# A batch of two for the first layer norm, with TensorE transposes and a newly searched order, in a two-layer linear-attention and GLU kernel

## The chip, the cores and the metric

The kernel runs on one core of one Trainium2 chip. The metric is device time in microseconds (us). A profile gives the *span* of one execution, about 2 us less than its time. Engines: PE is TensorE (PEld its weight loads), DVE is VectorE, ACT is ScalarE, POOL is GpSimd, SP issues transfers.

## The reference, cut to what matters

Four blocks in turn on a 2048 x 512 input: linear attention (A), a gated GLU (B), A, B, each behind a layer norm and with a residual. Only the first layer norm and the k-stage of the first A concern us.

```python
x = A_x                                          # [1, 2048, 512], bf16
x = x + _A_ref(_layernorm(x), A_wqkv, A_w_phi, A_wo)
x = x + _B_ref(_layernorm(x), B_W_gate, B_W_up, B_W_down)
...                                              # the same A and B once more
# in _A_ref, with 32 heads of 16:
pk = einsum("bhsd,hdf->bhsf", k, w_phi)
phi_k = concatenate([softmax(pk), softmax(-pk)])
kv = einsum("bhsf,bhsd->bhfd", phi_k, v)         # a sum over the whole sequence
```

The sum over the sequence is the point: until phi_k of all 2048 rows (16 tiles of 128) is there, no output of the attention can be made. The masked copy of kv, called *the KV matrix* below, ends the k-stage.

## The kernel before: the parts that matter

Every operation is recorded with what it reads and writes; a static order per engine (`ORDER`, found by an offline search) says which stands where, and `CHOICE` which engine takes an operation that could run on two. An engine works through its list in order, waiting on semaphores, so an operation that waits holds all behind it.

```python
for t in range(4):
    ldx(t, t + 1)                    # tiles 0 to 3, one load each
...
first = [r("x", 3)]                  # later loads wait until tile 3 has landed
ldx(4, 8, first)
ldx(8, 12, first)
...

def ln_stats(self, ts, tag):         # statistics of the tiles ts
    for t in ts:
        op("dve", ... e.bn_stats(k.stats6[:, t, :], k.x_sb[:, t, :]) ...)
        op("dve", ... e.bn_aggr(k.mv[:, t, :], k.stats6[:, t, :]) ...)
    # one "rv" and one reciprocal root for all of ts, on POOL
    op("pool", ... rv1[:, t0:t1] = var + eps ...)
    op("pool", ... rstd[:, t0:t1] = rv1 ** -0.5 ...)

def ln(self, t, tag, on_act=False, pe_bank=None, stats=True, copy_act=False):
    ...                              # ytile = x * rstd + nmr, on DVE or ACT
    if pe_bank is None:              # transpose by DMA
        self.dma_tr(... e.dma_start_transpose(k.yT[:, :, t*128:(t+1)*128], k.ytile[:, yb, :]) ...)
        return
    for c in range(NC):              # or four TensorE transposes into PSUM
        op("pe", ... e.transpose(pv[:, c*128:(c+1)*128], k.ytile[:, yb, c*128:(c+1)*128], k.ident[:]) ...)
    self.op2("act" if copy_act else "dve", ... copy of pv to yT ...)

def L(st):                           # a slab of four tiles
    self.ln_stats(tiles(st), "L0")
    for t in tiles(st):
        self.ln(t, "L0", on_act=t % 2, stats=False)
```

Tiles 0 to 3 are transposed on TensorE (`pe_bank` given), tiles 4 to 15 by DMA. After its tile is projected, k goes through two exponentials on ACT, a sum and a reciprocal on DVE (`Zk`, `rZk`), a product on POOL (`phik`), and is accumulated on TensorE (`kvacc`). TensorE fills waiting time with 70 dummy matmuls.

The softmax here doesn't subtract the row's maximum and nothing guards it: scores larger than these inputs give would overflow.

Of the kernel before, what the change touches and what calls it, by code (L numbers as in the profile page):

```python
# [14 lines left out]
        "29 26 6 25 27 28 2a 2b 4t 2c 39 49 3u 4y 4e 44 5i 5n 58 5s 4j 6j 6k 67 73 72 8l 6d 84 6a 4o 83 8k 91 9x 9y 7r 96 9z c4 c5 9b c6 9g d9 da db b4 f9 f8 "  # L15
        "fm fl ay ee ef b2 eg gz gy fz h0 hx hw fy ij g5 g4 ik gb ga gg gh ii hv mk mj n4 n3 mu mt lm lq lt ne nd nn no nt r8 o5 o4 rf of op oq jv kn p0 pa pb "
        "vg pl pw pv vk q6 qg qh qr s1 ko sd sc sn xw xt sx sy t8 lg tt tj ti zn u4 ue u3 zu up uo uz wd wo wp x9 wz xa m8 ru ym yn xk z7 11o z8 yx 10k 11s zi "
        "10l 11v 10v 142 w2 12t yb 149 146 134 13p 135 13f 109 159 14z 13q 15a 15u 12a 15v 15k 14o 16x 178 177 17i 1b7 16m 18l 1aw 1c9 1db 1ad 1by 1d0 1e6 1dv "
        "1ea 1f0 1fg 1ew 1em 1gj 1fw 1gk 1fc 1gi 1jm 1hk 1hl 1hj 1kb 1fs 1ib 1ic 1kr 1l7 1g8 1ia 1j2 1j3 1gx 1ll 1lk 1j1 1m9 1ma 1nv 1k6 1ob 1mz 1my 1lj 1or "
        "1l3 1kn 1p7 1nn 1m8 1mn 1no 1mx 1pl 1pk 1ly 1q9 1nm 1o7 1nc 1qa 1pj 1qz 1qy 1on 1rq 1rp 1q8 1s4 1p3 1qx 1s3 1py 1ro 1t5 1t6 1s5 1s6 1t8 1qn 1t7 1u7 "  # L20
        "1ua 1u8 1xr 1uw 1uv 1u9 1xx 1y3 1uy 1ym 1yn 1ux 1z1 1z2 1y9 1yl 1zh 1zg 1z0 1zv 1zw 1zf 24t 1zu 24u 255 24v 24w 256 258 230 257 25u 25t 25h 25i 25k "
        "25w 25v 25j 26q 271 27d 272 22j 27n 27c 27z 27o 27y 289 28a 28l 28k 28v 28w 297 29h 296 29i 29t 29s 2be 23c 23x 2bp 2bq 24i 2cc 2cb 2c1 26f 2c0 2dj "
        "2cn 2cm 2di 2dt 2b3 2e5 2du 2e4 2ef 2eg 2er 2eq 2ft 2fu 2hu 2i5 2i6 2ih 2ig 2j2 2ir 2j3 2a7 2is 2d7 2kg 2k6 2kh 2k5 2l2 2l3 2ks 2kr 2mh 2le 2mg 2ld "
        "2fi 2hb 2ju 2m5 2qa 2pz 2qb 2n8 2ql 2qw 2qx 2qm 2sa 2r7 2sl 2sb 2r8 2ny 2sw 2sx 2t7 2sm 2pg 2t8 2um 2tj 2ti 2ul 2g8 2rz 2mv 2ua 2vw 2x5 2ak 2v0 2xg "
        "2xr 2xh 2od 2y3 2xs 2y2 2vd 2yd 2yp 2ye 2yo 2z0 2zb 2yz 2zm 2za 2zl 2gl 2wo 2zw 2zx 308 2wb 307 30z 2oq 31c 30m 322 "),
    "dve": (
        "2z 30 33 3a 3b 3e 3l 3m 3v 3k 3w 3p 2m 53 3z 5d 5x 5z 5t 5v 5u 60 5y 5w 7i 7g 7f 7h 6l 64 6m ao 74 ap 75 an am 85 7t 86 8m a0 7x 8n 7v a3 a1 a4 c7 ca "
        "c8 cb dc df b0 fa dg fn dd fo fb eh ek el ei em h1 h2 fq h4 hy hz h5 i1 il im i0 in io j2 j1 j3 j4 ix jd iz je iy j0 k6 jj k7 ku ky l1 l2 jo l3 l4 jp "
        "l6 l7 lv lw ju kc ly lz nu kh rc rg ki rh og ld ri o6 le or p1 rk pc pm rl vn vo q7 m5 px vq qi m6 xp qs kp s2 vs so se r4 sz xy xz t9 rr tk tu y1 u5 "
        "uf uq zr 13s we lh v0 zw zx zy zz rs vc 13t vz x0 wq w0 y8 y9 xb yo xl 13v 106 107 17w yy 15x zj 15y m9 z9 17x 15z 10m 17y 1b9 1ba 19o 10w 12u 11y 181 "  # L30
        "19p 14c 120 121 136 118 14d 13g 16c 14e 16d 150 19r 1cb 127 11k 13r 15b w3 128 1cc 18b 18c 15w 15l 1cd 14l 14m 16y 16j 16k 17j 179 17v 18i 18j 1a3 1a4 "
        "1bo 1bp 19b 1cq 1cr 18z 1aa 1ab 1b8 1dl 1ax 1dm 19n 1bv 1cx 1bw 1cy 1ca 1e8 1ds 1dt 1e7 1eb 1dc 1ey 1fe 1f3 1fh 1d1 1en 1ex 1jk 1kp 1fu 1fx 1gl 1fj "
        "1ft 12b 1k9 1fd 1l8 1ks 1gy 1dw 1hm 1g9 1hn 1j4 1j5 1gm 1id 1ha 1go 1nt 1l5 1nw 1mb 1ie 1i1 1hp 1mc 1la 1o9 1is 1k7 1jj 1p5 1oc 1gn 1os 1op 1ko 1p8 "
        "1lm 1ln 1n0 1ig 1n1 1n2 1l4 1lo 1pm 1lz 1lp 1nd 1np 1mo 1j7 1nq 1pn 1po 1r0 1pp 1r1 1o8 1r3 1qb 1qc 1s7 1s8 1oo 1p4 1rr 1rs 1se 1sf 1pz 1qo 1t9 1tg "
        "1rf 1xp 1ta 1th 1qe 201 1xs 1sw 1xv 202 203 20f 1xu 1ty 1tl 204 20g 1y1 208 209 1yo 1um 1y7 1y6 1yp 1z3 1ya 1yq 1z4 1yc 1zi 1zj 1zl 1zx 1zy 200 1zz "
        "20a 21r 21q 21s 21p 20d 221 222 227 22u 22v 22c 23n 23o 22d 20m 22i 248 249 235 236 265 23b 20n 2et 26r 266 2gm 2eu 24f 23u 23v 273 2ev 27e 2gn 280 "
        "28b 27p 2at 24g 2au 28m 2go 2lg 298 2cx 29j 28x 29u 2cy 2j5 26c 2j6 26d 2n9 2na 2f8 2f9 2bf 23d 2a6 2lh 2br 2aj 2li 2ll 2b0 2h1 2cd 2c2 2h2 2d4 2ff "
        "2co 23y 2b1 2or 2os 2dk 2nc 2d5 2fg 2e6 2eh 2dv 2es 2tl 2fv 2jk 2jl 2g7 2ra 2ou 2b4 2hv 2rb 2i7 2ow 2lv 2tm 2lw 2gk 2it 2h8 2h9 2ii 2j4 2no 2m2 2k7 "
        "2np 2rf 2m3 2jr 2js 2l4 2ki 2kt 2p6 2p7 2lf 2mi 2mu 2rp 2nv 2nw 2rq 2n7 2m6 2u0 2u1 2qc 2q0 2hc 2jv 2op 2oc 2vm 2pd 2qn 2qy 2pe 2r9 2sc 2rw 2rx 2vn "
        "2t9 2sn 2sy 2tk 2un 2uz 2u7 2u8 2vt 2vu 2vc 2x6 2xt 2ub 2xi 2wa 2yf 2wn 2y4 2yq 2s0 2zn 2z1 2zy 2zc 309 30l 30y 31b 31o 320 "),  # L40
    "pool": (
        "2p 0 1 4 2t 5 2w 2x 31 2 2u 2n 2o 32 3c 34 3d 3n 3o 2y 3x 3y 3f 2s 2r 2q 2v 61 62 66 63 69 6c 3 7j 7l 7k 7m 7n 7o 6n 7p 7q 76 ar aq as au at 87 av aw "
        "ax 8o a2 a5 c9 cc dh fp fc de fd ff ej h3 fs en h6 l5 lu lx rj jw vp jx vr vt xx kq y0 zv y2 100 13u 13x 17z li 11w rv 160 11x 14a 14b ma 162 19q 1bb "
        "1be 11z 10a yc 19t 14f 1bc yd 1cg rw w4 1ce 10b 18m 14p 1ec 16n 1ed 1f1 1f2 1fi 1fy 1fz 1jn 1kc 1kd 1bz 18n 16o 1ke 14q 1jo 1kt 1jp 1c0 1ku 1l9 1ae "
        "1ho 12c 1nx 1p9 1dx 1pa 1if 1od 1md 1ny 1oe 1ot 1j6 1d2 1ou 1me 1n3 1af 1r2 1nr 1ns 1sg 1sj 1s9 1sc 1rt 1qd 1sa 1tb 1te 1tc 1xt 206 1sh 1ti 1tj 20h "
        "1y4 1y5 20k 1xy 1xz 1y0 1ru 1yr 1yb 1z6 1z5 1zk 20i 20b 20o 20r 20p 2ew 2gr 2gp 22k 22l 2ey 2j7 2j8 23e 26g 2ja 24j 2nb 24k 23z 2lj 2ot 2b5 2tn 2to "
        "2tq 2d8 26h 2ne 2rc 2rd 2d9 2hd 2fj 2fk 2nz 2o0 2jw 2vx 2ph 2m7 2s1 2pi 2uc 2vy "),
    "pe": (
        "7 8 9 a b c d e f g h i j k 4p 4q 4r 4s l m n o p q r s t u v w x y z 35 36 37 38 10 11 12 13 14 15 16 17 3g 3h 3i 3j 18 45 46 47 48 3q 3r 3s 3t 4z 50 "
        "51 52 59 5a 5b 5c 4u 4v 4w 4x 4a 4b 4c 4d 40 41 42 43 5e 5f 5g 5h 4f 4g 4h 4i 5j 5k 5l 5m 19 1a 1b 54 55 56 57 1c 1d 1e 5o 5p 5q 5r 1f 1g 6f 6g 6h 6i "  # L50
        "1h 6y 6z 70 71 1i 1j 1k 1l 1m 1n 1o 8g 8h 8i 8j 1p 1q 1r 1s 6p 1t 1u 7z 80 81 82 1v 1w 6o 1x 1y 1z 20 21 22 23 24 4k 4l 4m 4n 9l 9m 9n 9o 8x 8y 8z 90 "
        "9h 9i 9j 9k 9p 9q 9r 9s 9t 9u 9v 9w 6q 6r 6s 6t 77 78 79 7a 92 93 94 95 bo bp bq br bs bt bu bv 6u 6v 6w 6x 97 98 99 9a 88 89 8a 8b bw bx by bz c0 c1 "
        "c2 c3 ct cu cv cw 9c 9d 9e 9f cx cy cz d0 d1 d2 d3 d4 d5 d6 d7 d8 f4 f5 f6 f7 fh fi fj fk 7b 7c 7d 7e 8c 8d 8e 8f 8p 8q 8r 8s dy dz e0 e1 a6 a7 a8 a9 "
        "e6 e7 e8 e9 e2 e3 e4 e5 ea eb ec ed fu fv fw fx ae af ag ah cd ce cf cg cl cm cn co 8t 8u 8v 8w aa ab ac ad gm gn go gp gi gj gk gl ai aj ak al ch ci "
        "cj ck gq gr gs gt gu gv gw gx di dj dk dl g0 g1 g2 g3 hn ho hp hq dq dr ds dt ia ib ic id cp cq cr cs dm dn do dp hr hs ht hu g6 g7 g8 g9 du dv dw dx "
        "es et eu ev eo ep eq er gc gd ge gf ie if ig ih mb mc md me mf mg mh mi f0 f1 f2 f3 ew ex ey ez h7 h8 h9 ha hf hg hh hi i2 i3 i4 i5 ip iq ir is hb hc "
        "hd he hj hk hl hm i6 i7 i8 i9 it iu iv iw j5 j6 j7 j8 j9 ja jb jc mz n0 n1 n2 mv mw mx my k2 k3 k4 k5 jf jg jh ji jy jz k0 k1 ml mm mn mo mp mq mr ms "
        "kr ks kt kv kw kx kz l0 jk jl jm jn lj lk ll ln n5 n6 n7 n8 lo lp lr ls n9 na nb nc nf ng nh ni nj nk nl nm jq jr js jt k8 k9 ka kb r5 r6 r7 r9 np nq "
        "nr ns kd ke kf kg ob oc od oe o0 o1 o2 o3 nw nx ny nz ra rb rd re o7 o8 o9 oa ol om on oo oh oi oj ok l9 la lb lc os ot ou ov kj kk kl km p6 p7 p8 p9 "
        "p2 p3 p4 p5 vd ve vf vh ow ox oy oz m1 m2 m3 m4 pr ps pt pu pd pe pf pg pn po pp pq ph pi pj pk vi vj vl vm py pz q0 q1 q8 q9 qa qb q2 q3 q4 q5 qc qd "  # L60
        "qe qf qj qk ql qm xm xn xo xq rx ry rz s0 qn qo qp qq qt qu qv qw qx qy qz r0 r1 r2 r3 s8 s9 sa sb s4 s5 s6 s7 sf sg sh si xr xs xu xv sj sk sl sm sp "
# [295 lines left out]
ACT = mybir.ActivationFunctionType  # L357
# [19 lines left out]
CHOICE = {}  # L377
# [38 lines left out]
class Kernel:  # L416
# [96 lines left out]
    def setup(self):  # L513
        op, dma, r = self.op, self.dma, self.r
        k = self
# [698 lines left out]
```

## Time and profile before

| | |
|---|---|
| time, 3 executions | 379.43 us median (379.27 to 379.86) |
| span of the profiled one | 377.4 us |
| TensorE busy | 367.7 us, 97% of the span |
| statistic of tile 2 starts (DVE) | 6.94 us |
| first statistic of the second slab starts (DVE) | 10.99 us |
| KV matrix starts (DVE) | 53.07 us |

The prediction shows the busy tenths, the stretches and the waits. A line of a timeline gives start, duration, line, operation, output and input, count.

```profile
10.99 2.46 DVE L623 BATCH_NORM_STATS2 stats<-x_sb 128x6 f32<-128x512 bf16 x4
...
53.07 0.98 DVE L797 TENSOR_TENSOR kvbd<-ps,mask 128x136 bf16<-128x136 f32 x4
```

I call the first S and the second K. Between them VectorE has almost no wait; from K to the end of the span are 377.4 - 53.07 = 324.3 us.

### The profile page before, as it was taken

The numbers are of one execution on the slowest core, as the hardware profiler recorded it, in microseconds if no ns is written. First come the engines' busy times: TensorE is split into PE (matmuls) and PEld (weight loads), VectorE is DVE, ScalarE is ACT, GpSimd is POOL, SyncE is SP. The second block draws the span as 40 slices with busy tenths as digits, with TensorE's granted clock in tenths as the row PEclk, the third lists the DMA queues.
The fourth block names the chain that finished last, engine by engine and source line by source line (L and its number), as shares of the span: only waits on it lengthen the run. The fifth ranks groups of instructions, "written<-read, shape, count | busy, mean of one in ns | idle before, by whom it ended". The sixth has DMA issues, their size and how long they took to land.

```text
span 377.4 us, 6882 instructions
## 1 busy us (share of the span) xinstructions
PE 367.7 (97%) x2519; PEld 203.9 (54%) x2565; DVE 276.2 (73%) x607; ACT 227.0 (60%) x463; POOL 130.8 (35%) x234
## 2 busy tenths in 40 slices
PE   6999999999999999999999999999999999999997
PEld 5654555877744454454444446577664454445443
DVE  5999998989968676459799999898984654342323
ACT  3999878765744127874677568584635451653450
POOL 6799941133344001350463577023221201000020
PEclk9999999999999999999999999999999999999999
DMA  7632794313326444310300045335543442142012
GB/s 233 173 76 52 187 240 149 77 33 56 78 43 94 97 64 84 70 30 14 70 2 1 2 81 95 79 63 95 83 83 75 81 86 56 28 71 70 30 42 70
DMA packets 87856, 29.33 MB, mean 78 GB/s; under 512 B 79792, under 2 KB 86800, under 8 KB 87824
## 3 DMA queue, kind: packets, MB, share of 16 engines
q1 hardware_dynamic: 84368, 25.86, 33.7%
q10 hardware_dynamic: 3456, 3.05, 2.5%
q8 instruction: 20, 0.33, 0.4%
q14 instruction: 12, 0.10, 0.1%
HBM read 7.91 MB, written 2.10 MB: 27 GB/s over the span
## 4 chain that ended last, share of the span: by engine, by line
PE 85%; POOL 7%; DVE 3%; issue 2%; ACT 1%; DMA 1%; POOLq 0%; DVEq 0%
PE ps L962 37%; PE ps L1011 20%; PE ps L725 7%; PE ps L942 7%; POOL expk L750 5%; PE ps L822 5%; PE ps L988 3%; PE ps L921 2%; PE ps L787 1%; PE ps L886 1%; DMA hT<-in_A_wqkv_dram 1%; DVE Zk L744 1%; POOL rstd L648 1%; PE ps L868 1%; PE ps L539 0%
## 5 line engine op out<-in xcount | busy, mean ns | idle before, releaser
L962 PE MATMUL ps<-yT,Wgu 128*128 128x512 bf16 (+2 forms) x870 | 150.8, 320 | 0.6
L962 PEld LDWEIGHTS ps<-yT,Wgu 128*128 128x128 bf16 x880 | 78.5, 98 | 58.8 <-ACT expk L970 1.0
L964 ACT ACTIVATE gate_sb<-ps 128x512 bf16<-128x512 f32 (+2 forms) x110 | 50.7, 480 | 55.1 <-PE ps L962 41.8
L1011 PE MATMUL ps<-Wd,hT 128*128 128x512 bf16 (+4 forms) x354 | 79.3, 373 | 0.5
L1011 PEld LDWEIGHTS ps<-Wd,hT 128*128 128x128 bf16 (+1 forms) x363 | 34.6, 98 | 39.5 <-DVE hT L972 0.7
L972 DVE TENSOR_TENSOR hT<-gate_sb,expk 128x512 bf16<-128x512 bf16 (+2 forms) x70 | 23.9, 361 | 30.4 <-ACT expk L970 21.4
L970 ACT ACTIVATE expk<-ps 128x512 bf16<-128x512 f32 (+2 forms) x70 | 32.0, 475 | 22.2 <-PE ps L962 19.5
L710 ACT ACTIVATE sq<-x_sb,nmr 128x512 bf16<-128x512 bf16 x48 | 34.6, 721 | 10.3 <-DVE x_sb L687 6.6
L744 DVE TENSOR_REDUCE Zk<-expk 128x64 f32<-128x1024 bf16 x32 | 38.1, 1203 | 1.0 <-ACT expk L737 0.7
L714 POOL TENSOR_TENSOR rstd<-rv,mone 128x1 f32<-128x1 f32 x32 | 18.6, 589 | 50.2 <-DVE rv L712 50.0
L1013 DVE SCALAR_TENSOR_TENSOR x_sb<-ps,rstd,x_sb 128x512 bf16<-128x512 f32 (+2 forms) x33 | 23.9, 728 | 16.1 <-PE ps L1011 13.5
L942 PE MATMUL ps<-wo_p,oT 128*128 128x512 bf16 x118 | 30.8, 379 | 0.6 <-DVE oT L413 0.3
L975 DVE TENSOR_TENSOR hT<-gate_sb,ps 128x512 bf16<-128x512 bf16 (+2 forms) x40 | 21.7, 544 | 12.6 <-ACT gate_sb L964 6.4
L855 POOL TENSOR_TENSOR expq<-expq,rho 128x256 bf16<-128x256 bf16 x36 | 22.2, 624 | 24.4 <-DVE rho L852 23.7
L847 DVE TENSOR_REDUCE Zq<-expq 128x64 f32<-128x1024 bf16 x24 | 28.8, 1204 | 0.8 <-POOL rho L852 0.5
L687 DVE SCALAR_TENSOR_TENSOR x_sb<-ps,x_sb 128x512 bf16<-128x512 f32 x32 | 21.9, 687 | 8.6 <-PE ps L942 7.8
L750 POOL TENSOR_TENSOR expk<-expk,rZk 128x1024 bf16<-128x1024 bf16 x13 | 25.9, 2005 | 0.6 <-DVE rZk L746 0.6
L755 POOL TENSOR_TENSOR expk<-expk,rZk 128x512 bf16<-128x512 bf16 x17 | 19.1, 1134 | 11.8 <-DVE rZk L746 11.5
L822 PE MATMUL ps<-Wqp,yT 128*128 128x512 bf16 x91 | 22.8, 379 | 0.3
L725 PE MATMUL ps<-Wkp,yT 128*128 128x512 bf16 x84 | 22.0, 379 | 0.2
L725 PE MATMUL ps<-wv_p,yT 128*128 128x512 bf16 x85 | 21.9, 379 | 0.2
L712 POOL TENSOR_SCALAR rv<-rv 128x1 f32<-128x1 f32 x22 | 4.3, 203 | 45.3 <-ACT sq L710 45.3
(126 smaller groups left out, 514.1 us busy)
## 6 DMA issues: line engine op xcount, KB each, us to landing
out_dram<-x_sb ACTq DMA_DIRECT2D x15, 128.0 KB, 1.7
x_sb<-in_A_x_dram SPq DMA_DIRECT2D x3, 512.0 KB, 5.0
Wgu<-in_B_W_up_dram SPq DMA_DIRECT2D x4, 344.0 KB, 5.5
Wgu<-in_B_W_gate_dram SPq DMA_DIRECT2D x4, 344.0 KB, 4.3
Wd<-in_B_W_down_dram SPq DMA_DIRECT2D x5, 256.0 KB, 3.3
yT<-ytile SPq DMA_TRANSPOSE x56, 2.5
qT<-expq SPq DMA_TRANSPOSE x40, 2.5
x_sb<-in_A_x_dram SPq DMA_DIRECT2D x4, 128.0 KB, 3.6
```

What stands on the lines that cost most here:

```text
L710: op("act", lambda e: e.activation(k.sq[:], k.x_sb[:, t, :], ACT.Square, scale=-float(D), bias=k.nmr[:, t, :], accum_out=k.rv1[:, t, :]), ...
L725: op("pe", (lambda ic, bank, W: lambda e: e.matmul(k.pb[bank][:], k.yT[:, ic, t * 128:(t + 1) * 128], W[:, ic, :], start=(ic == 0), stop=( ...
L744: op("dve", lambda e: e.tensor_reduce(k.Zk[:, zb, :], k.expk[:, t, :, :, :].rearrange("p g s (h f) -> p (g s h) f", f=16), AX.X, ALU.add), ...
L750: op("pool", lambda e: e.tensor_tensor(kv, kv, k.rZk[:, rb, :].unsqueeze(2).to_broadcast([P, 64, 16]), ALU.mult), [r("expk", t, 0), r("exp ...
L822: op("pe", (lambda ic, bank, tt: lambda e: e.matmul(k.pb[bank][:], k.yT[:, ic, tt * 128:(tt + 1) * 128], k.Wqp[:, ic, :], start=(ic == 0), ...
L847: op("dve", lambda e: e.tensor_reduce(k.Zq[:, b, :], k.expq[:, t, :, :, :].rearrange("p g s (h f) -> p (g s h) f", f=16), AX.X, ALU.add), ...
L942: op("pe", (lambda c, bank: lambda e: e.matmul(k.pb[bank][:], k.oT[:, ob, c, :], k.wo_p[:, c, :], start=(c == 0), stop=(c == NC - 1)))(c, ...
L962: op("pe", (lambda bank, W, ic, fc, Mf: lambda e: e.matmul(k.pb[bank][0:Mf, 0:n], W[:, ic, fc * 128:fc * 128 + Mf], k.yT[:, ic, c0:c0 + n] ...
L964: op("act", (lambda Mf, gb, gs: lambda e: e.activation(k.gate_sb[0:Mf, gs, 0:n], k.pb[gb][0:Mf, 0:n], ACT.Relu))(Mf, gb, gs), [self.RP[gb] ...
L970: op("act", (lambda Mf, ub, up: lambda e: e.activation(up[0:Mf, 0:n], k.pb[ub][0:Mf, 0:n], ACT.Copy))(Mf, ub, up), [self.RP[ub]], ru, 170 ...
L972: op("dve", (lambda Mf, up, gs, u: lambda e: e.tensor_tensor(k.hT[0:Mf, u, 0:n], k.gate_sb[0:Mf, gs, 0:n], up[0:Mf, 0:n], ALU.mult))(Mf, u ...
L1011: op("pe", (lambda fc, Kf, u, c0, bank, m0, m1: lambda e: e.matmul(k.pb[bank][:, m0:m1], k.hT[0:Kf, u, c0:c0 + 128], k.Wd[0:Kf, fc, m0:m1] ...
```

## The change

Its intent is to get TensorE's real work started sooner: tiles 4 and 5 get their statistics as a batch of two, a load of their own and TensorE transposes; and the search that fixes the order was run anew, with ScalarE's queue allowed to issue loads during compute.

```diff
-        ldx(4, 8, first)
+        ldx(4, 6, first)
+        ldx(6, 8, first)
...
         def L(st):
-            self.ln_stats(tiles(st), "L0")
-            for t in tiles(st):
-                self.ln(t, "L0", on_act=t % 2, stats=False)
+            for ts in ([[4, 5], [6, 7]] if st == 1 else [tiles(st)]):
+                self.ln_stats(ts, "L0")
+                for t in ts:
+                    self.ln(t, "L0", on_act=t % 2, stats=False, pe_bank=(7 if t == 4 else 6) if t < 6 else None, copy_act=t == 5)
```

Cut: the new `ORDER` and `CHOICE` (all engines' lists; 51 small operations go from POOL to DVE, 43 back, ten copies between DVE and ACT), the cost that the search books for a table load, and a choice of engine for some normalizations.

## The prediction

> **What bounds the kernel now.** I read the page's rows of busy tenths first, then its chain of waits, then busy time by stretch, the waits by engine, and the timeline of the first 60 us. Each digit below is one fortieth of the span (9.4 us).
>
> ```profile
> PE   6999999999999999999999999999999999999997
> DVE  5999998989968676459799999898984654342323
> ACT  3999878765744127874677568584635451653450
> POOL 6799941133344001350463577023221201000020
> ...
> PE 85%; POOL 7%; DVE 3%; issue 2%; ACT 1%; DMA 1%; POOLq 0%; DVEq 0%
> ```
>
> TensorE is the bound from end to end except at the start: there are four full engines in slices 2 to 5, and the 7% of POOL in the chain lies there. Busy time by stretch (the columns are window, length, then PE, PEld, DVE, ACT, POOL with counts, clock, DMA share, GB/s) says the same in microseconds:
>
> ```profile
> 0.00:20.00 20.00, 16.47 (x149) 11.48 (x152) 15.05 (x34) 13.28 (x23) 14.93 (x45) 1.00 0.68 197
> 20.00:60.00 40.00, 38.73 (x313) 20.59 (x318) 38.72 (x61) 35.32 (x51) 30.83 (x29) 1.00 0.66 160
> 60.00:370.00 310.00, 307.60 (x2029) 169.09 (x2064) 219.99 (x510) 178.42 (x391) 85.03 (x161) 1.00 0.31 59
> 370.00:377.40 7.40, 4.93 (x33) 2.75 (x32) 2.47 (x4) 0.00 (x0) 0.00 (x0) 1.00 0.27 89
> ```
>
> After 60 us TensorE has 2.4 us of gaps in 310, so nothing that reorders other engines can win more than that there; the last 7.4 us are the last down-projection, its residual and the store. From 20 to 60 us I count work instead of busy time. The groups list 141 matmuls of 512 columns, 144 of 68, 20 of 128 and 8 of 144; the chain gives 24 of 512 columns in 5.18 us, 0.216 each, and the timeline about 0.035, 0.056 and 0.06 for the others: 30.5 + 5.0 + 1.1 + 0.5 = 37 us, and about 38 with the five matmuls missing from the trace (313 matmuls against 318 weight loads). So TensorE, too, is nearly full there.
>
> The slack is before 20 us, where 70 dummy matmuls on a tile of ones fill 7.6 us. They end where the first transposed tiles of the second slab arrive:
>
> ```profile
> 18.93 0.62 PE L539 MATMUL ps<-ones 128*128 128x128 bf16 x8
> 19.38 1.03 PE L725 MATMUL ps<-wv_p,yT 128*128 128x512 bf16 x4
> 20.25 1.03 PE L766 MATMUL ps<-Wkp,yT 128*128 128x512 bf16 x4
> ```
>
> L539 is the dummy; from L725 on TensorE has real work. Whatever brings the end of the dummies forward, and lets the other three engines follow, shortens the kernel. What holds it there: VectorE waits for input, then everybody is in a row.
>
> ```profile
> DVE stats L623 <- DMA x_sb<-in_A_x_dram: 4.4, 2, 3.6
> ...
> POOL rv L630 <- DVE mv L625: 2.8, 3, 0.9
> POOL expk L750 <- DVE rZk L746: 0.6, 1, 0.6
> ```
>
> (From the waits of DVE and of POOL before 55 us: total, times, longest.) VectorE waits 3.6 us for tile 0 and 0.85 us for tile 2, which lands only at 6.94 us; after that it has no wait worth naming until 53 us, when the masked KV matrix is made. POOL's last wait for a statistic ends at 13.82 us (rv of tiles 4 to 7, one batch of four), and its first normalization of k starts at 18.46.
>
> **What the Trainium skill says.** "VectorE: DVE Perf Modes", section "The three transpose paths", gives 390 ns for a 128x128 transpose on TensorE and 1309 ns by DMA. The trace agrees in kind, not in size: four TensorE transposes (a whole 128x512 tile) take 0.40 us, 0.056 us apart, while a DMA transpose of a tile occupies its queue 1.19 us and lands after 2.5. "TensorE: Matmul & The Clock Gate", section "Part 4: PE-mode transpose", says that the result goes to PSUM and needs a copy: here 0.42 us on DVE or 0.60 on ACT. "DMA: Bandwidth & Descriptors", section "Issuing engines are not separate DMA queues", says that loads issued from another engine run on the same 16 DMA engines, so only issue time is saved; the trace has both queues sharing 343 to 384 GB/s in the first microseconds, and an issue takes 0.33 to 0.5 us.
>
> **The change part by part.**
>
> *Batch of two.* The statistics of tiles 4 and 5 get their own reciprocal root. Removed: waiting for two more tiles, that is two statistics (0.61 us apart) and two aggregations, about 1.4 us sooner for tiles 4 and 5. Added on POOL: one more rv (0.24) and one more rstd (1.04 for a batch of four; 1.0 assumed for two), 1.25 us.
>
> *Own load.* The four-tile load becomes two; one more issue on SP (about 0.4 us), free. In the kernel before VectorE did not wait for that load, so this alone gains nothing.
>
> *TensorE transposes.* Two DMA transposes leave (2 x 1.19 us of queue, 2.5 us to landing). Eight TensorE transposes come, 8 x 0.056 = 0.45 us in a stretch where dummies ran, plus 0.42 on DVE and 0.60 on ACT. The time from normalized tile to transposed tile falls from 2.5 us to about 0.4 + 0.5 = 0.9, 1.6 us less.
>
> *Search.* The static order shows no load moved to another queue; only the order moved. The ACT queue now sends wk0, wv1, wk1, wv0 before the table load, and wv2, wv3, wk2, wk3 later; before, all but wk3 went out by 4.2 us. So seven loads rather than eleven compete with the four x tiles, and tile 2 is issued before tile 3. I expect tile 2 about 1 us earlier. Also 51 small operations go from POOL to DVE and 43 back, nearly all after 55 us. In the saturated stretch: one weight copy goes from DVE to ACT (0.42 off, 0.60 on), rho 0 and nrx 0 go from POOL to DVE (about 0.4 on).
>
> **Sum by engine, up to the end of the k-stage at 53 us.**
> - DVE: full from 6.94 on. Starts about 1.0 to 1.3 us sooner, given back 0.4 of rho and nrx; the two copies cancel. Net 0.6 to 0.9 sooner.
> - POOL: rv of tiles 4, 5 at about 13.82 - 1.4 - 1.0 = 11.4. From there to the first normalization of k stand, in the new order, rv, rstd, four nmr, rv, rstd, the padded-tile memset (0.83), eight aggregation steps with a root (about 2.9): 6.8 us, so 18.2 instead of 18.46, but now with the root of tiles 8 to 11 (1.02) already behind it. The second normalization comes at about 20.4 instead of 21.61. Some 1.2 us sooner, if VectorE's reciprocals keep up.
> - ACT: the chain from the second v copy (11.29) can start about 1 us sooner, gets 0.60 for the tile-5 copy and 0.60 for the weight copy, and one v copy of 0.5 is postponed. Net about 0.7 to 1.0.
> - PE: the dummies could end near 17 instead of 19.4, but k of tile 3 (4 x 0.216 = 0.86) now stands after them: 1.0 to 1.5 sooner.
>
> The slowest of the four counts, VectorE: 0.6 to 0.9 us; I take 0.9, because all others allow more and TensorE's gaps between 20 and 60 leave some to win. After 60 us the same work at the same pace, +/-0.3 for the reshuffle. So 379.43 - 0.9, rounded to 378.4 with the small favour of a search that placed the rest anew.
>
> **The rivals.**
> - *Hidden anyway:* ACT, DVE and POOL are 88 to 100% busy between 20 and 50 us, so an earlier transposed tile only queues behind them, and the 1.25 us on POOL and 1.0 us of copies eat the gain. For it: VectorE's full row. Against: the gain also comes from earlier x tiles, ahead of the full row. It would make 379.2 to 379.8.
> - *A new wait on weights:* wk2, wk3, wv2 and wv3 are sent 1 to 2 us later; the first v projection (7.5 us) needs all of wv and might start near 8.5, pushing compositions of Wk and the first exponentials. For it: loads took 4.2 to 4.6 us to land. Against: with fewer in flight they land faster, and the new order puts that projection later. It would make about 380.
> - *More than expected:* the whole 1.6 us of transpose latency and the 1.4 us of batching show, as TensorE's real work starts by 17 us. It would make 377. Against: DVE.
>
> **Range and chances.** The three rivals span 377 to 380; 377.0 to 379.8 should hold it 8 times in 10. 2% is 7.6 us, and all TensorE dummies together are 7.6 us with input loading among them, so over 2% faster is next to excluded; over 2% slower would need a stall that the check of order gives no hint of. Chances 0.01, 0.98, 0.01.
>
> **What would show it.** In the profile after: the statistic of tile 2 starting near 6 us; POOL's first batch rv near 11.5; the first L750 step near 18.2 and the second near 20.4; the last dummy near 17; the masked KV matrix near 52.2 instead of 53.07; the stretch from there to the end equally long. I am wrong if VectorE's start isn't earlier, if ACT shows a wait for weight transposes between 6 and 12 us, or if the k-stage ends sooner and TensorE then waits more after 60 us.

## The result, and the profile after

The changed kernel takes 379.50 us (median of 4, 379.42 to 379.76); the kernel before beside it 379.44. The ratio is 1.0001, with a 95% interval of 0.9984 to 1.0019: the same. Ratios are the mean time of one kernel's fast runs over that of the other's in the same rounds, so not quite the ratio of the medians.

The page of the changed kernel, busy tenths by fortieths of the span and the chain that ended last:

```profile
PE   7999999999999999999999999999999999999997
...
DVE  5899998987998657458988988998985464353223
ACT  4999967875524616964677567685524632653460
POOL 7699950242232000613753358011310150001200
...
PE 93%; ACT 2%; DVE 2%; DMA 1%; issue 0%; POOL 0%; POOLq 0%
```

That last line seems to say that POOL left the path and that TensorE alone is left. I don't read it so, because the experiments below show that work added to POOL or VectorE still costs. Where several engines are full, a small shift is enough to hand the chain from one to another. The stretches, as in the prediction:

```profile
0.00:20.00 20.00, 17.21 (x160) 12.62 (x161) 14.23 (x34) 13.68 (x24) 14.19 (x44) 1.00 0.76 192
20.00:60.00 40.00, 38.91 (x316) 20.30 (x314) 38.94 (x62) 34.87 (x51) 31.44 (x29) 1.00 0.64 163
60.00:370.00 310.00, 309.09 (x2065) 168.81 (x2066) 222.83 (x520) 178.14 (x389) 79.74 (x156) 1.00 0.30 58
```

TensorE's and VectorE's sums from 20 to 60 us are within 0.25 us of those before. But VectorE (the third sum) did only 14.23 us of work by 20 us, where it had done 15.05. Where that went is in its timeline:

```profile
5.82 0.69 DVE L625 BATCH_NORM_STATS2 stats<-x_sb 128x6 f32<-128x512 bf16 x1 [0.61 <-DMA x_sb<-in_A_x_dram]
...
7.80 0.41 DVE L675 TENSOR_SCALAR ytile<-x_sb,mv,rstd 128x512 bf16<-128x512 bf16 x1 [0.25 <-POOL rstd L633]
...
9.72 0.41 DVE L675 TENSOR_SCALAR ytile<-x_sb,mv,rstd 128x512 bf16<-128x512 bf16 x1 [0.44 <-POOL rstd L633]
...
11.41 1.28 DVE L625 BATCH_NORM_STATS2 stats<-x_sb 128x6 f32<-128x512 bf16 x2 [0.95 <-DMA x_sb<-in_A_x_dram]
...
53.76 1.00 DVE L802 TENSOR_TENSOR kvbd<-ps,mask 128x136 bf16<-128x136 f32 x4
```

In brackets is the idle time before the instruction and what ended it. Tile 2 is there 1.1 us sooner, as hoped. Then VectorE waits for the root of tile 2, for the root of tile 3, and for the load of tiles 4 and 5, 1.64 us in all. S is 11.41, later than before, and K is 0.7 us later. POOL's batch and its first product follow:

```profile
13.00 0.23 POOL L632 TENSOR_SCALAR rv<-mv 128x2 f32<-128x2 f32 x1 [1.48 <-DVE mv L627]
13.32 0.71 POOL L633 TENSOR_TENSOR rstd<-rv,mhalf 128x2 f32<-128x2 f32 x1
...
20.01 1.93 POOL L755 TENSOR_TENSOR expk<-expk,rZk 128x1024 bf16<-128x1024 bf16 x1
21.89 0.20 POOL L651 TENSOR_TENSOR nmr<-agg,rstd 128x4 f32<-128x4 f32 x1
22.08 1.93 POOL L755 TENSOR_TENSOR expk<-expk,rZk 128x1024 bf16<-128x1024 bf16 x1
```

This profile fell on the slowest of the four executions (spans 377.5, 377.6, 377.7 and 377.8), which matters for the 0.95.

### The profile page after: what moved, and what is told of

It reads as the page before. It is cut to its first block, busy times and chain, and to the rows that moved or that the text cites. A ratio compares the mean times of both kernels' runs of the same rounds, so it can differ in the third digit from the quotient of the medians.

```text
span 377.8 us, 6939 instructions
## 1 busy us (share of the span) xinstructions
PE 370.6 (98%) x2573; PEld 204.6 (54%) x2573; DVE 278.5 (74%) x618; ACT 226.7 (60%) x462; POOL 125.4 (33%) x228
## 4 chain that ended last, share of the span: by engine, by line
PE 93%; ACT 2%; DVE 2%; DMA 1%; issue 0%; POOL 0%; POOLq 0%
PE ps L967 37%; PE ps L1016 20%; PE ps L730 8%; PE ps L947 7%; PE ps L827 5%; PE ps L771 4%; PE ps L993 3%; PE ps L792 2%; PE ps L926 2%; PE ps L873 1%; PE ps L540 1%; DMA hT<-in_A_wqkv_dram 1%; PE ps L891 1%; ACT expk L742 1%; ACT expk L774 0%; DVE expk L760 0%
## 5 line engine op out<-in xcount | busy, mean ns | idle before, releaser
L1016 PE MATMUL ps<-Wd,hT 128*128 128x512 bf16 (+3 forms) x363 | 80.1, 373 | 0.0
L947 PE MATMUL ps<-wo_p,oT 128*128 128x512 bf16 x128 | 32.8, 379 | 0.3 <-DVE oT L414 0.3
L760 POOL TENSOR_TENSOR expk<-expk,rZk 128x512 bf16<-128x512 bf16 x20 | 22.0, 1110 | 15.7 <-DVE rZk L751 15.0
L860 POOL TENSOR_TENSOR expq<-expq,rho 128x256 bf16<-128x256 bf16 x26 | 16.3, 633 | 25.3 <-DVE rho L857 22.6
L717 POOL TENSOR_SCALAR rv<-rv 128x1 f32<-128x1 f32 x26 | 5.4, 211 | 57.8 <-ACT sq L715 57.8
L827 PE MATMUL ps<-Wqp,yT 128*128 128x512 bf16 x96 | 23.8, 379 | 0.0
```

The costliest lines, as they stand in the source:

```text
L827: op("pe", (lambda ic, bank, tt: lambda e: e.matmul(k.pb[bank][:], k.yT[:, ic, tt * 128:(tt + 1) * 128], k.Wqp[:, ic, :], start=(ic == 0), ...
L947: op("pe", (lambda c, bank: lambda e: e.matmul(k.pb[bank][:], k.oT[:, ob, c, :], k.wo_p[:, c, :], start=(c == 0), stop=(c == NC - 1)))(c, ...
L1016: op("pe", (lambda fc, Kf, u, c0, bank, m0, m1: lambda e: e.matmul(k.pb[bank][:, m0:m1], k.hT[0:Kf, u, c0:c0 + 128], k.Wd[0:Kf, fc, m0:m1] ...
```

## The experiments

**A ruler first.** I read S, K and the span in the trace of every run. "End - K" came out nearly constant in all kernels with the new order, whatever was done to them in the k-stage, so in these kernels K tells the time of the traced execution. One trace is one execution, though, and not always a typical one.

| run | median us | ratio to before (95%) | S | K | K - S | span | end - K |
|---|---|---|---|---|---|---|---|
| before | 379.43 | | 10.99 | 53.07 | 42.08 | 377.4 | 324.3 |
| changed | 379.50 | 1.0001 (0.9984 to 1.0019) | 11.41 | 53.76 | 42.35 | 377.8 | 324.0 |
| a_x45_early | 379.48 | 1.0002 (0.9990 to 1.0014) | 10.49 | 53.10 | 42.61 | 377.1 | 324.0 |
| a_w_early | 379.08 | 0.9991 (0.9979 to 1.0003) | 10.57 | 53.61 | 43.04 | 377.7 | 324.1 |
| a_dmatr | 378.67 | 0.9978 (0.9965 to 0.9990) | 10.68 | 52.76 | 42.08 | 376.9 | 324.1 |
| a_batch4 | 380.45 | 1.0029 (1.0015 to 1.0043) | 12.01 | 55.44 | 43.43 | 379.5 | 324.1 |
| a_dmatr_batch4 | 379.96 | 1.0017 (1.0004 to 1.0030) | 10.64 | 53.73 | 43.09 | 377.8 | 324.1 |
| a_best | 378.55 | 0.9973 (0.9960 to 0.9987) | 10.53 | 52.56 | 42.03 | 376.6 | 324.0 |
| a_dve_plus | 380.90 | 1.0038 (1.0024 to 1.0051) | 10.54 | 54.95 | 44.41 | 378.9 | 324.0 |
| a_pe_plus | 380.85 | 1.0032 (1.0019 to 1.0046) | 11.12 | 53.77 | 42.65 | 377.8 | 324.0 |
| a_pool_plus | 380.03 | 1.0013 (1.0001 to 1.0025) | 10.48 | 54.14 | 43.66 | 378.1 | 324.0 |
| a_copy4_act | 379.52 | 1.0002 (0.9990 to 1.0015) | 11.13 | 53.58 | 42.45 | 377.6 | 324.0 |
| b_batch2 | 380.06 | 1.0017 (1.0005 to 1.0030) | 10.79 | 53.27 | 42.48 | 377.8 | 324.5 |
| a_best2 | 378.75 | 0.9987 (0.9972 to 1.0002) | 10.84 | 52.92 | 42.08 | 377.0 | 324.1 |

After K the kernels with the new order are 0.2 to 0.3 us shorter (324.0 to 324.1 against 324.3, and 324.5 for the run with the old order and a batch of two; the old order has only these two traces). All else happens before K. All runs were correct.

**a_x45_early: the load of tiles 4 and 5 doesn't wait.** First theory: the gain was lost to that load's late landing.

```diff
-        ldx(4, 6, first)
+        ldx(4, 6)
```

> The changed kernel with one edit: the load of tiles 4 and 5 no longer waits for tile 3 to land, so it is issued right after the small phi load (about 3.1 us instead of 6.43). In the changed kernel VectorE waits 0.95 us for it, until 11.41 us. Theory 1 (the expected gain was lost to that late landing): the wait goes, VectorE's full stretch starts 0.9 us sooner, the masked KV matrix is made 0.4 to 0.9 us before 53.76 us, and the time falls by the same, to 378.6 to 379.1. Rival (the stage is bound by TensorE and the sum of work on the other engines, so the landing is hidden anyway): the wait goes, the matrix stays at 53.6 to 53.9, time 379.3 to 379.6.

The wait of 0.95 us is gone in the trace and K is 0.66 us earlier, but the time is 379.48 (the mean span at full clock 377.35, against 377.65 for the changed kernel's four). So the landing is worth at most about 0.3 us of the 0.4 to 0.9 that I forecast, and the theory falls as the main cause. The landing differs from execution to execution: with the same loads in the same order the wait was 0.95 (changed), 0.62 (a_copy4_act) and 0.56 (a_pe_plus), and absent in a_dmatr, a_dmatr_batch4, a_dve_plus and a_pool_plus. Why it differs is open.

**a_w_early: the weights go out early again.** Edit in ScalarE's list alone:

```diff
-wk0 wv1 wk1 wv0 table (copy wk0) wv2 wv3 (copy x0) wk2 wk3
+wk0 wv1 table wk1 wv0 wv2 wv3 wk2 (copy wk0) wk3 (copy x0)
```

> The changed kernel with the ACT queue's eight weight loads issued as early as in the kernel before (all but one ahead of the first copy, the table load between them) and nothing else moved. Theory 1a (the late weights, 5.1 to 6.9 us, compete with the load of tiles 4 and 5 and make it take 5.0 us): with them out of the way that load takes 3.5 to 4.2 us and VectorE's wait of 0.95 us shrinks to 0 to 0.3; but tile 2 lands later, near 6.9 instead of 5.82. Time 378.9 to 379.4. Rival (the landing is late because it is issued only at 6.43 us, after tile 3): the load still lands at 11 us or later, time 379.4 to 380.0.

Tile 2 came as early as with late weights (6.00), so the late weights are not what brought it; issuing tile 2 ahead of tile 3 is what is left, and no run tests that by itself. The wait for tiles 4 and 5 was gone, but VectorE then waited 0.84 us for tiles 8 to 11. The time, 379.08, can't be told from before, but it is 0.4 less than that of the changed kernel. Where the 0.4 comes from stays open: the traced execution (379.62) is the slowest of the five, the other four lie between 378.94 and 379.10.

**A two-by-two: transposes and batch.** a_dmatr puts the DMA transposes back, a_batch4 the batch of four, a_dmatr_batch4 both.

```diff
 # a_dmatr
-    self.ln(..., pe_bank=(7 if t == 4 else 6) if t < 6 else None, copy_act=t == 5)
+    self.ln(..., pe_bank=None)          # two DMA transposes back in SP's list
 # a_batch4
-for ts in ([[4, 5], [6, 7]] if st == 1 else [tiles(st)]):
+for ts in [tiles(st)]:
```

> The changed kernel with tiles 4 and 5 transposed by DMA again (the two TensorE transposes and their two copies taken out, the two DMA transposes put back in the place they have in the kernel before); batch of two, own load and order stay. If the transposes on TensorE bring anything (1.6 us less latency, as I reckoned), dummies end later and the time rises by 0.5 to 1.0, to 380.0 to 380.5. If they are worth nothing because 0.4 us on VectorE and 0.5 us on ScalarE are given back, 379.2 to 379.6.

> The changed kernel with one batch of four for the statistics of tiles 4 to 7 again (one rv and one root instead of two each), transposes, loads and order as changed. If the batch of two brings its 1.4 us of earlier normalization to the path, taking it away costs 0.4 to 1.0: 379.9 to 380.5. If it is only paid for on POOL (0.94 us more) and hidden otherwise, the first normalization of k comes 0.5 to 0.9 us sooner and the time is 378.9 to 379.5.

> The changed kernel with both undone: DMA transposes for tiles 4 and 5 and one batch of four; own load and the new order stay. The fourth cell of a two-by-two: changed 379.5, DMA transposes alone put back 378.7, batch of four alone put back 380.4. Theory 2 (TensorE transposes cost 0.3 to 0.8 because VectorE is full from the first statistic of tile 4 to the masked KV matrix; the batch of two gains because it lets normalization start): the two effects add, 379.4 to 379.8. Rival (the batch of two only repairs what the early TensorE transposes need, since k of tiles 2 and 3 stand behind them in TensorE's order): without TensorE transposes the batch doesn't matter, 378.5 to 379.0.

| median us | batch of two | batch of four |
|---|---|---|
| TensorE transposes | 379.50 (changed) | 380.45 |
| DMA transposes | **378.67** | 379.96 |

So the two named parts of the change pull apart. In the new order the batch of two wins 1.0 to 1.3 us, and the TensorE transposes lose 0.5 to 0.8. The table also closes the sum: the new order and loads without either part take 379.96, 0.5 more than before; the batch of two brings 378.67, and the transposes give that back. I had expected taking the transposes out to cost time or nothing; it is what beats the kernel before. Two of the six executions of a_batch4, the traced one among them, and one of the five of a_dmatr_batch4, had a short loss of clock (see the end). The means without these are 379.55 and 380.17 in the upper row, 378.70 and 379.84 in the lower: the batch then wins 0.6 to 1.1 and the transposes lose 0.3 to 0.9, so the signs stand and the sizes are rough.

**a_best and where a copy goes.** DMA transposes, early load of tiles 4 and 5, and one operation moved up so that the root of tile 3 is ready in time:

```diff
 # VectorE's list
-stats 3, apply 1, apply 2, aggr 3, ...
+stats 3, aggr 3, apply 1, apply 2, ...
```

> A version meant to beat both: the changed kernel with DMA transposes for tiles 4 and 5, the aggregation of tile 3 moved up to stand right after its statistic (so that POOL's root of tile 3 is ready when VectorE normalizes tile 3; VectorE waited 0.44 us for it), and the load of tiles 4 and 5 not waiting for tile 3. If VectorE's full stretch sets the end, it starts 0.4 to 0.6 us sooner than in the run with DMA transposes alone: 378.0 to 378.4. If some other engine sets it, 378.6 to 378.9.

378.55 us, ratio 0.9973: better than both kernels by 0.9 us, and not to be told from a_dmatr (378.67). Against a_x45_early it differs by the transposes and that one move, and up to the first sum of exponentials the two traces are level. VectorE in a_x45_early:

```profile
16.29 1.20 DVE L749 TENSOR_REDUCE Zk<-expk 128x64 f32<-128x1024 bf16 x1
17.68 0.42 DVE L414 COPY yT<-ps 128x512 bf16<-128x512 bf16 x1 [0.19 <-PE ps L683]
18.02 0.68 DVE L625 BATCH_NORM_STATS2 stats<-x_sb 128x6 f32<-128x512 bf16 x1
...
53.10 1.00 DVE L802 TENSOR_TENSOR kvbd<-ps,mask 128x136 bf16<-128x136 f32 x4
```

and in a_best:

```profile
16.34 1.20 DVE L749 TENSOR_REDUCE Zk<-expk 128x64 f32<-128x1024 bf16 x1
17.46 0.68 DVE L625 BATCH_NORM_STATS2 stats<-x_sb 128x6 f32<-128x512 bf16 x1
...
52.56 1.00 DVE L802 TENSOR_TENSOR kvbd<-ps,mask 128x136 bf16<-128x136 f32 x4
```

The copy out of PSUM sets VectorE back by 0.56 us at once (18.02 against 17.46), 0.34 of work and 0.19 of waiting for the transposes, and 35 us later K is still 0.54 us behind. Nothing absorbs it. The moved aggregation won little: in place of the waits for roots (0.25 and 0.44) VectorE now waits 0.58 us for transposed weights, and S went from 10.68 to 10.53 only.

**a_copy4_act: the same copy on ScalarE.**

```diff
-copy_act=t == 5      # tile 4's copy on DVE
+copy_act=t < 6       # both copies on ACT, tile 4's behind "apply 7"
```

> The changed kernel with one edit: the copy of tile 4's transpose out of PSUM stands on ScalarE, behind the normalization of tile 7, instead of on VectorE. In the traces with and without TensorE transposes VectorE runs level up to the first sum of exponentials (16.29 against 16.34 us) and is 0.57 us behind from the copy on (0.19 waiting for the transposes, 0.34 of copy), and stays so to the masked KV matrix (53.10 against 52.56). Theory 2 (that copy on the full engine is the cost of the transposes): time 378.7 to 379.0, nearly all of the 0.8 us that the DMA transposes win. Rival (ScalarE and TensorE are as full; 0.5 us more on ScalarE costs the same): 379.3 to 379.7.

379.52: nothing won. The waits of VectorE from 10 to 54 us in this run:

```profile
DVE Zk L749 <- ACT expk L774: 0.4, 1, 0.4
DVE Zk L749 <- ACT expk L742: 0.2, 1, 0.2
```

The 0.34 us of copy and the wait before it have become 0.6 us of waiting for ScalarE's exponentials. My theory that the cost lies in VectorE's copy alone falls. ScalarE is nearly as full (40.2 us of work in the 42.35 between S and K of the changed kernel, VectorE 42.2), so that either engine can pass the delay on.

A rival that I left untested is TensorE's own row. In a_x45_early:

```profile
17.26 0.39 PE L683 MATMUL ps<-ident,ytile 128*128 128x128 bf16 x4
17.48 1.03 PE L730 MATMUL ps<-Wkp,yT 128*128 128x512 bf16 x4
...
20.13 1.03 PE L771 MATMUL ps<-Wkp,yT 128*128 128x512 bf16 x4
```

and in a_best:

```profile
16.99 1.03 PE L730 MATMUL ps<-Wkp,yT 128*128 128x512 bf16 x4
...
19.64 1.03 PE L771 MATMUL ps<-Wkp,yT 128*128 128x512 bf16 x4
```

L683 is the transpose, L771 the first product of the second slab. All versions have the same 70 dummies, so the eight transposes take no dummy's place: they come on top, and TensorE is 0.49 us behind already at 17.48, before VectorE's copy starts. In a_copy4_act that product starts at 20.07, still late, which could by itself be why moving the copy won nothing. No run separates the copy from the transposes, for instance by leaving out dummies.

**Which engine is the bound?** Work that nobody needs, added in the middle of the stretch: two statistics on VectorE (1.2 us), four matmuls on TensorE (0.86), two zero-fills on POOL (1.0).

```diff
         kv(6, 2)
+        for i in range(2):                      # a_dve_plus; a_pool_plus: h10t memset
+            op("dve", ... e.bn_stats(stats6[:, 11, :], x_sb[:, 11, :]) ...)
...
+                for i in range(4 if (nm, tt) == ("v", 7) else 0):      # a_pe_plus
+                    op("pe", ... e.matmul(k.pb[bank][:], ..., start=True, stop=True) ...)
```

> The changed kernel with two more statistics of tile 11 on VectorE (about 0.61 us each, result not used), behind the sixth tile's sum of exponentials, so in the middle of the stretch in which all four engines look full. Theory 2 (VectorE sets the end of the stretch): the masked KV matrix comes 1.1 to 1.3 us later and the time rises by as much, to 380.6 to 380.9. Rival (TensorE sets it: the chain of waits gives TensorE the whole of 24 to 49 us): rise below 0.5.

> The changed kernel with four more matmuls of 512 columns on TensorE (4 x 0.216 = 0.86 us) ahead of v of tile 7, each overwritten by the matmul that starts the group. Rival (TensorE sets the stretch): the masked KV matrix comes 0.8 to 0.9 us later and the time is 380.3 to 380.5. Theory 2 (VectorE sets it and TensorE's work in it has a little slack): the matrix moves by less than 0.4; but TensorE is full after 60 us, so work pushed behind the matrix can still cost: 379.5 to 380.4, and the matrix's time is what tells.

> The changed kernel with two more zero-fills of the padded tile on POOL (0.52 to 0.83 us each by their traces), behind the normalization of k of tile 5, in the middle of the stretch where POOL is 95 to 100% busy. VectorE +1.2 us cost 1.2 to 1.4 us, TensorE +0.86 cost about 1.2, half a microsecond moved from VectorE to ScalarE changed nothing. If POOL is as binding (its added root for the batch of two is then a real cost): 380.3 to 380.9. If POOL follows VectorE with slack (the added root was hidden): 379.4 to 379.9.

Against the changed kernel's 379.5, VectorE's 1.2 us cost 1.4, TensorE's 0.86 about 1.3 at the median, and POOL's 1.0 cost 0.5. So no one engine is the bound alone: work added to VectorE or TensorE comes out in full at the median. TensorE's case has a loose end. Its traced execution has a span of 377.8, no cost at all; the other three have 378.8, 379.1 and 379.1. No trace of a slow one was kept, so how its 0.86 us becomes 1.3 is open. POOL's half may be too little, since the landing of tiles 4 and 5 differs between executions. The traces of a_pool_plus and a_x45_early agree within 0.02 us from S up to the zero-fills at 34 us, and there the two fills (1.05 us) come out in full: K at 54.14 against 53.10, span 378.1 against 377.1. So POOL's added root for a batch of two need not have been hidden; that root itself was not tested.

**b_batch2: the batch of two in the kernel before.** Statistics of 4 and 5 first, two roots, and the normalizations of both moved up by hand in the old order; everything else as before.

> The kernel before with the batch of two alone: statistics of tiles 4 and 5 ahead of 6 and 7, two roots on POOL instead of one, normalization of tile 4 ahead of the last statistic and of tile 5 ahead of the first exponentials; loads, DMA transposes and all other order as before. In the changed kernel's order the batch of two was worth 1.3 us with DMA transposes (378.7 against 380.0). If that is a worth of its own: 378.0 to 378.6. Theory 2 (VectorE is full from 10.99 us to the masked KV matrix at 53.07 in the kernel before with 0.22 us of waits, so earlier normalization can't shorten it; the 1.3 us is only what the new order loses when the batch it was made for is taken away): 379.1 to 379.6.

380.06, slower than before by 0.6. What was worth 1.0 to 1.3 us in the new order costs in the old one. VectorE's waits from 4 to 54 us, of which the kernel before has 0.22 for `Zk`, are as few as there (0.29); there was nothing to win, and the added root and the moved normalizations push the first exponentials (15.41 against 15.01) and K (53.27) back. I read the gain in the two-by-two as what the new order loses when the batch that it was built around is taken out; a search of the old order with a batch of two, which might place it better than I did by hand, was not made.

**a_best2: early weights and no waiting for tiles 4 to 7 on top of a_best.**

> A second version meant to beat both: the first one (DMA transposes, aggregation of tile 3 moved up, load of tiles 4 and 5 not waiting), with the eight weight loads sent as early as before and the load of tiles 6 and 7 not waiting either. In the first version VectorE's full stretch started at 10.53, held by 0.58 us of waiting for the weight transposes of the third slice. If its start sets the end, it now starts at 10.0 to 10.2 and the time is 377.9 to 378.3. If the loads now collide (tile 2 or tiles 8 to 11 later, as in the run with early weights, where VectorE waited 0.84 us for tile 8), 378.4 to 379.0.

378.75, not better than a_best. The loads seem to collide: tile 2 comes at 6.26 instead of 5.87, and VectorE still waits 0.5 us for transposed weights. S is 10.84. In every version without a landing wait, a_batch4 with its loss of clock aside, S lies between 10.5 and 10.8: each wait that I removed ahead of it gave way to another.

## Why the prediction was right or wrong

The measured 379.5 us lies in the range (377.0 to 379.8) and the class, same, is right. The gain of 0.9 us that the centre rested on is not there, and the rival "hidden anyway" (379.2 to 379.8) gives the number. That the range held is owed to its width, 2.8 us for rivals of opposite sign, and not to the mechanism: the centre, 378.4, is 1.1 us off, and a gain and a loss that I had not seen cancel. The rival's reasons hold in part. The transposed tiles 5 and 4 are there at 16.94 and 18.76, but they queue: the first product of the second slab starts at 20.13 instead of 20.25. Of my signs of being wrong the first came true: VectorE's full stretch starts no earlier.

- **Right:** tile 2 about 1 us earlier (6.94 to 5.82). No load changes its queue. After 60 us the same length within 0.3 (end - K is 0.3 shorter).
- **Wrong in its cause:** that fewer loads in flight bring tile 2. With the weights early it came at 6.00. (The count was off, too: by 4.2 us four weight loads stand in the new trace and seven in the old, so eight loads with the x tiles against eleven, the small phi load aside.)
- **Failed step, "Starts about 1.0 to 1.3 us sooner":** VectorE's full stretch started 0.4 us *later* in the profile and 0.3 to 0.5 sooner in seven of the eight variants with the new order, full clock and no landing wait (0.15 in a_best2). I took the arrival of tile 2 for the start of the stretch. Between them stand waits for two of POOL's roots (0.25 and 0.44), which a removed wait exposes, and a landing of tiles 4 and 5 of which I had said that VectorE "did not wait for that load". It hadn't when it started at 10.99; asked 0.5 us sooner, it sometimes does.
- **Failed step, "the two copies cancel":** the weight copy that leaves VectorE stood ahead of S, where VectorE in the changed kernel waits 1.64 us anyway; the copy of tile 4 that comes stands in the full stretch. Time saved on a waiting engine doesn't make up for time added to a full one: 0.56 us with its wait, and 0.54 still at K.
- **Failed step, ScalarE "0.7 to 1.0" sooner and so with room:** its first exponential starts at 15.21 against 15.01, later and not sooner, and moving half a microsecond there bought nothing. The step's own terms (1 us sooner, 0.60 and 0.60 added, 0.5 postponed) leave only 0.3.
- **Failed step, TensorE "1.0 to 1.5 sooner":** I had the dummies end where the tiles of the second slab arrive, and the transposes run where dummies ran. The list places the dummies and keeps all 70; the first thing after them in the lines shown, L725, is still a product of the first slab. The dummies end 1.0 us sooner (18.57 against 19.55), and with k of tile 3 behind them the second slab starts 0.12 us sooner.
- **Mis-sized term:** the root for two columns took 0.71 us, not the 1.0 that I assumed, so the split costs POOL 0.6 us and not 1.25. But rv came at 13.00 instead of 11.4, because the statistics came late, and the first product at 20.01 instead of 18.2. (From rv to there it took 7.0 us; the terms that I had summed to 6.8 make 7.2.)
- **The marks** (first product of POOL near 18.2, second near 20.4, last dummy near 17, KV matrix near 52.2) were missed on each count: 20.01, 22.08, 18.35, 53.76. A misreading without consequence: the 384 GB/s of "the first microseconds" stands at 10 us, and between them it falls to 202.

In short: shown are a loss of 0.3 to 0.9 us from the TensorE transposes, and a batch of two that wins 0.6 to 1.3 us in the order made for it and costs 0.6 where it was put into the old one by hand; two traces of the old order also show 0.2 to 0.3 us won after K. In the traces the earlier tiles are spent on new waits ahead of S. Which engine turns the transposes into a loss, through the copies or through TensorE's row, stays open.

## What to carry to other kernels

When several engines are full in the same stretch, look for the time at which the fullest one becomes full and the time at which the stretch ends, and judge each part of a change by these two. A shorter latency that is paid for with work on full engines can be a loss: the DMA transpose, slow as it is, takes no time of a compute engine in these traces. And undo the parts of a bundled change one by one, since two that cancel look exactly like two that do nothing.

## What the Trainium skill lacked or had wrong

- "VectorE: DVE Perf Modes", section "The three transpose paths", gives 390 ns on TensorE and 1309 ns by DMA for one 128 x 128 block, and its section "Rules for kernel authors" advises TensorE where PSUM will do as the destination. Here a tile of four such blocks takes 0.40 us on TensorE and lands after 2.5 us by DMA; yet the TensorE path lost 0.3 to 0.9 us for two tiles, so the advice needs the condition that TensorE, and the engine that makes the copy, have room.
- "TensorE: Matmul & The Clock Gate", section "Part 1: The HAM clock gate (the "warmup" mystery)", says that TensorE goes back to half clock after at least one idle window of about 3.4 us, and further down that short idles between groups of matmuls do it as well if they come often enough; how often it does not say. The trace of a_batch4 is of the second kind: the longest idle stretch between 2 and 10 us is 1.23 us, and TensorE is busy for 0.55 of the 2 us from 6 us on (the first sum below).

```profile
6.00:8.00 2.00, 0.55 (x8) 0.37 (x8) 1.74 (x5) 1.15 (x2) 0.88 (x3) 1.00 0.85 224
8.00:10.00 2.00, 1.59 (x10) 0.95 (x12) 1.51 (x6) 0.60 (x1) 1.28 (x3) 0.65 0.79 251
10.00:12.00 2.00, 2.00 (x12) 1.29 (x11) 0.71 (x2) 1.12 (x2) 1.59 (x5) 0.50 0.99 279
12.00:14.00 2.00, 2.00 (x20) 1.26 (x19) 2.00 (x7) 1.26 (x4) 0.00 (x0) 0.99 1.35 309
```

  The third number from the end is the granted clock. No limit shows here: the trace of a_x45_early has the same 0.55 us in the same 2 us, with an idle stretch of 1.32 us, and keeps full clock. 5 of 61 executions of kernels with the new order had a mean clock of 0.995 or 0.996 and were 1.1 to 1.7 us longer than the mean of the others of their kernel; none of the 32 of the kernel before, run beside them, had. The new order has 12 dummies between the first weight transposes and the second tile's, the old one 23; whether that is the reason was not tested.
- No page gives the time of POOL's power by columns: mostly 0.57 us for one (0.56 to 0.86 in the first layer norm), 0.71 for two, 1.04 for four.
